# A new order for the work of an attention and gated feed-forward kernel, and a later place for one weight load

## The chip, the cores and the metric

The kernel runs on one core of a Trainium2 chip. A core has five engines that run side by side and meet through semaphores: TensorE (PE in the profile) multiplies matrices and writes to PSUM banks, VectorE (DVE) and ScalarE (ACT) move and change what lies there or in the core's memory, GpSimd (POOL, "Pool" here) does the same without access to PSUM, and SyncE (SP) issues most of the transfers. Pool, SP and ScalarE each have a queue of transfers; all of them run on the same 16 DMA engines. The metric is the device time of one execution, in microseconds (us).

## What is computed

Attention over 4 batches and 8 heads, 768 positions, head size 64, in which each query sees at most six chunks of 32 keys, and behind it a gated feed-forward layer:

```python
k_chunks = k.reshape(B, H, nc, chunk, D)
k_min, k_max = np.min(k_chunks, axis=3), np.max(k_chunks, axis=3)
ub = np.sum(np.maximum(q[:, :, :, None, :] * k_min[:, :, None], q[:, :, :, None, :] * k_max[:, :, None]), axis=-1)
ub = np.where(causal, ub, -1e9)
top_chunks = np.argsort(ub, axis=-1)[..., -6:]        # six chunks by an upper bound of their scores
scores = np.where(selected & not_ahead, q @ k.T / sqrt(D), -1e9)
x = softmax(scores) @ v                               # then heads side by side: 3072 x 512
out = (sigmoid(x @ w_gate) * (x @ w_val)) @ w_out     # 512 -> 1536 -> 512
```

Inputs and outputs are float32; the products run in float16.

## The kernel before

The 24 blocks of 128 query rows (four batches of six) are cut into eight **units** u0 to u7 of three blocks, 384 rows. u0 has the first blocks of batches 0 to 2 (operations named with f: `kfT_0`, `scf_0`, `expf_0_0`, `cmf_0_0`, `pvf_0_0`); each later unit has its own chain:

- keys and queries are loaded (`k0_u2`, `q0_u2`), cast or rearranged (`kn`, `qn`), turned by TensorE (`kT`, `qT`), and copied out as keys (`kt`, `hk`), queries (`qf`, `hq`), positive parts of the queries (`qm`) and smallest and largest keys of each chunk (`kx`, `kcr`);
- `ub` computes the bounds, `ubn`, `mx`, `ap`, `apt` find the sixth largest, `hqm` writes the choice beside the queries;
- `sc` scores, `exp` the exponential, `cm` the causal mask on Pool (line 1014, for u0 `cmf`, line 746), `pv` the product with the values, `rz` and `x` the division, `xps` and `xT` the turn to the layout of the next layer;
- the feed-forward layer: `g` gate products, `tanh` for the sigmoid, `v` value products, `hg` their product, `o` the output product, `osb` its way out of PSUM, `out` the store. From u2 on, the gate and value products are done with seven products of half size instead of eight; for that, **sums of weight blocks** (`ss0_g0` and so on, line 1213) and of the activations (`tt`, line 1226) are needed. Units 4 to 7 do likewise for the output (`tw`, `sw`, `p1` to `p7`).

While the chain of one unit computes bounds and scores, TensorE works on the feed-forward products of the unit before, so the two run interleaved.

What sets the order is written out by hand as three tables. `ORDER` lists all 2013 operations, each with its engine: P TensorE, A ScalarE, V VectorE, G Pool, S SP. Each engine runs its own operations in this order; an operation waits only for what it reads, and for buffers to be free. `SLOTS` gives each buffer its place in memory or its PSUM bank. `TIES` holds pairs `a<b`: operation a (nearly always one of Pool) also waits for the end of b. The tables are used at the end of the kernel:

```python
for op in plan.order():
    op.emit(op.engine)
    for b in ties.get(op.name, ()):
        tc.add_manual_dep(traced[n], ends[b], ..., reason="tie")
```

The weights are loaded by Pool's queue, which casts them to float16. The gate weights come in thirds `wg0` to `wg2`; of the first third, the first quarter of its rows comes alone, earlier, as `wgp` (line 603), so that three gate products of u0 (`ga_u0_0` to `ga_u0_2`) can begin before the rest, `wg0` (line 605), has landed. Between, `fl` are products of ones that keep TensorE running where it has nothing to do. Pool's order at the start is: `epat`, copies of the pattern of chunks into the key buffers (`hkp010`, `hkp100`), `wgp` between these two, then `v10`, the cast `v16_0_0` of the first values (`vf_0`), the masks `cmf_0_0`, `cmf_0_1`, `cmf_1_0`, the cast `vc_1` of the values `vf_1`, `cmf_1_1`, `hkf0`, and then `wg0` and `wv0`.

Of the kernel before, what the change touches and what calls it, by code (L numbers as in the profile page):

```python
# [118 lines left out]
xps_u1_1=P xT_u1_1=A exp_u1_4_2=A hg_u0_6=V hk1_u1_3=V hg_u0_5=V v_u0_8=P g_u0_10=P tanh_u0_10=A kcr1=V hg_u0_10=V g_u0_8=P tanh_u0_8=A  # L119
hg_u0_8=V sc_u1_5_2=P exp_u1_5_2=A g_u0_9=P tanh_u0_9=A hg_u0_9=V sc_u1_4_0=P exp_u1_4_0=A cm_u1_1=G pv_u1_1=P cm_u1_0=G qn_u2_2=G  # L120
sc_u1_5_0=P pv_u1_0=P exp_u1_5_0=A sc_u1_6_1=P exp_u1_6_1=A sc_u1_6_2=P exp_u1_6_2=A exp_u1_5_1=A sc_u1_7_2=P sc_u1_7_0=P g_u0_11=P
qT_u2_2=P sc_u1_7_1=P tanh_u0_11=A exp_u1_7_2=A exp_u1_7_0=A exp_u1_7_1=A kn_u2_1=V kT_u2_1=P rz_u1_0=V x_u1_0=V xps_u1_0=P cm_u1_5=G
pv_u1_5=P cm_u1_4=G pv_u1_4=P qf_u2_2=V q3_u2=S qn_u2_1=V qT_u2_1=P sc_u1_6_0=P kt_u2_1=A exp_u1_6_0=A kn_u2_0=G kT_u2_0=P kt_u2_0=A
v_u0_11=P rz_u1_2=V xT_u1_0=V x_u1_2=V xps_u1_2=P q0_u2=S qn_u2_3=G qT_u2_3=P cm_u1_7=G pv_u1_7=P kx0_u2_0=V o0_u0_0=P o1_u0_0=P
hg_u0_11=V kx1_u2_1=V kx1_u2_0=V cm_u1_6=G pv_u1_6=P rz_u1_3=V x_u1_3=V k2_u2=S qn_u2_0=A qT_u2_0=P o0_u0_1=P xps_u1_3=P xT_u1_3=V
qf_u2_1=A hq0_u2_2=A qf_u2_3=A qm_u2_1=G hq1_u2_1=G k3_u2=S kn_u2_2=G hk1_u2_0=A xT_u1_2=A kT_u2_2=P kn_u2_3=A kT_u2_3=P qf_u2_0=V
# [131 lines left out]
p3z_u67=P e12_u67=A out_u67_0=S  # L258
# [1259 lines left out]
```

## Time and profile before

| | us |
|---|---|
| median of three runs | 273.23 (271.15 to 276.38) |
| the profiled execution | 272.19 |
| its span, first to last instruction | 270.5 |
| busy: TensorE | 261.6 (97%) |
| busy: VectorE | 226.3 (84%) |
| busy: ScalarE | 208.7 (77%) |
| busy: Pool | 181.7 (67%) |

Busy is the union of an engine's instructions in one profiled execution. A matmul's record reaches from its start to the arrival of its last result, so records of neighbours overlap, and a busy TensorE need not be at its full pace. "Idle before" stands with an instruction whose engine did nothing ahead of it, together with what ended the wait. DMA issues on Pool count in its timeline with the time of issuing; the landing comes later. The time of an execution is a little longer than the span, by 1.69 us in the profiled one.

### The profile page before, as it was taken

Reading aid. Unit: us, or ns where it says so; the run is one execution under the profiler, and the core shown is the slowest. Engines: PE = TensorE matmul, PEld = TensorE weight load, DVE = VectorE, ACT = ScalarE, POOL = GpSimd, SP = SyncE. Lnnn points to the kernel's source line nnn. Section 1 sums busy time; section 2 is a strip of 40 time slices with the busy share of each in tenths; the row PEclk is TensorE's granted clock in tenths of the full one; section 3 lists DMA queues with packets and bytes.
Section 4 is the critical chain, followed back from the end, with each engine's and each line's share of the span. In section 5 each row is a group of like instructions: output and inputs, shape, how many; then the busy total and the mean of one; then the engine's idle time right before and its main releaser. Section 6 shows DMA issues by size and latency. Waiting matters only on the chain.

```text
span 270.5 us, 8392 instructions
## 1 busy us (share of the span) xinstructions
PE 261.6 (97%) x3180; PEld 213.1 (79%) x3180; DVE 226.3 (84%) x612; ACT 208.7 (77%) x397; POOL 181.7 (67%) x269
## 2 busy tenths in 40 slices
PE   6888999999999999999999999999999999999994
PEld 4565667656666689886799888889989999999984
DVE  4789946688999999998999998988886889888652
ACT  6269778699999999998988998999976775654221
POOL 5787744677998999867999368476548436770531
PEclk9999999999999999999999999999999999999999
DMA  6999999999999993996955541410100300100236
GB/s 153 228 263 207 203 213 215 235 194 176 188 182 165 212 221 78 185 170 113 204 128 127 135 92 23 130 54 16 33 18 17 82 2 2 40 2 2 78 120 234
DMA packets 131577, 34.76 MB, mean 129 GB/s; under 512 B 119760, under 2 KB 128464, under 8 KB 131536
## 3 DMA queue, kind: packets, MB, share of 16 engines
q1 hardware_dynamic: 125728, 29.24, 51.3%
q0 software_dynamic: 4768, 4.72, 10.4%
q8 instruction: 25, 0.41, 0.7%
q10 hardware_dynamic: 1040, 0.26, 0.4%
q14 instruction: 16, 0.13, 0.1%
HBM read 30.67 MB, written 6.29 MB: 137 GB/s over the span
## 4 chain that ended last, share of the span: by engine, by line
PE 91%; DMA 4%; SPq 1%; POOL 1%; issue 0%; ACT 0%; DVE 0%; POOLq 0%
PE bank L1242 31%; PE bank L991 13%; PE bank L1290 12%; PE bank L1373 11%; PE bank L1135 10%; PE bank L1030 7%; PE bank L912 3%; DMA wg<-in_moe_w_gate_dram 3%; PE bank L702 1%; DMA arena<-in_q_dram 1%; SPq L629 1%; PE bank L788 1%; PE bank L739 0%; POOL arena L746 0%; PE bank L1065 0%
## 5 line engine op out<-in xcount | busy, mean ns | idle before, releaser
L1008 ACT ACTIVATE arena<-bank 128x1024 f16<-128x1024 f32 (+5 forms) x120 | 84.4, 749 | 5.7 <-PE bank L991 4.4
L1242 PE MATMUL bank<-arena 128*128 128x192 f16 x432 | 50.5, 246 | 0.0
L1308 DVE SCALAR_TENSOR_TENSOR arena<-arena,bank 128x384 f16<-128x384 f16 x78 | 41.5, 544 | 10.2 <-ACT arena L1304 4.8
L1125 POOL TENSOR_TENSOR arena<-arena 128x256 f16<-128x256 f16 x39 | 25.4, 669 | 29.8 <-DVE arena L1125 9.5
L1304 ACT ACTIVATE arena<-bank 128x384 f16<-128x384 f32 x78 | 37.4, 493 | 9.2 <-PE bank L1242 4.9
L1014 POOL TENSOR_SCALAR_AFFINE_SELECT arena<-arena 128x384 f16<-128x384 f16 (+1 forms) x56 | 27.5, 503 | 16.7 <-ACT arena L1008 8.5
L1242 PEld LDWEIGHTS <-arena 128*128 128x128 f16 x432 | 36.5, 98 | 2.8 <-issue 0.6
L1373 PE MATMUL bank<-wo,arena 128*128 128x512 f16 x144 | 36.0, 379 | 0.0
L1242 PE MATMUL bank<-arena,wv 128*128 128x192 f16 x288 | 34.0, 246 | 0.0
L1242 PE MATMUL bank<-arena,wg 128*128 128x192 f16 x288 | 32.6, 246 | 0.0
L1030 PE MATMUL bank<-v,arena 128*128 128x65 f16 x640 | 26.8, 193 | 0.0
L991 PE MATMUL bank<-hqo,hko 128*128 128x128 f16 (+2 forms) x220 | 26.5, 243 | 0.0
L991 PE MATMUL bank<-hqe,hke 128*128 128x128 f16 (+2 forms) x220 | 26.4, 243 | 0.0
L1135 PEld LDWEIGHTS <-arena 128*128 128x128 f16 x252 | 24.4, 98 | 2.4
L1030 PEld LDWEIGHTS <-arena 128*128 128x128 f16 x640 | 24.5, 97 | 1.6 <-issue 0.5
L1242 PEld LDWEIGHTS <-wg 128*128 128x128 f16 x288 | 24.3, 98 | 1.6 <-issue 0.4
L1242 PEld LDWEIGHTS <-wv 128*128 128x128 f16 x288 | 24.2, 98 | 1.8 <-issue 0.2
L440 ACT COPY arena<-bank 128x384 f32<-128x384 f32 (+3 forms) x44 | 19.4, 450 | 5.9 <-PE bank L1242 2.7
L1257 DVE TENSOR_TENSOR bank<-bank,arena 128x384 f32<-128x384 f32 x36 | 20.2, 562 | 4.3 <-ACT arena L1304 2.2
L1226 POOL TENSOR_TENSOR arena<-arena 128x384 f16<-128x384 f16 x20 | 18.2, 912 | 6.0 <-DMA arena<-arena 4.3
L1257 DVE TENSOR_TENSOR arena<-bank,arena 128x384 f32<-128x384 f32 x36 | 19.8, 551 | 2.4 <-PE bank L1242 2.1
L1373 PEld LDWEIGHTS <-arena 128*128 128x128 f16 x144 | 13.4, 98 | 10.3
(124 smaller groups left out, 555.8 us busy)
## 6 DMA issues: line engine op xcount, KB each, us to landing
arena<-in_v_dram SPq DMA_DIRECT2D x26, 256.0 KB, 4.0
out_dram<-arena SPq DMA_DIRECT2D x24, 256.0 KB, 2.2
arena<-in_k_dram SPq DMA_DIRECT2D x12, 384.0 KB, 5.6
arena<-in_q_dram SPq DMA_DIRECT2D x12, 384.0 KB, 5.9
arena<-in_q_dram SPq DMA_DIRECT2D x12, 128.0 KB, 5.7
arena<-in_k_dram SPq DMA_DIRECT2D x12, 128.0 KB, 4.2
wv<-in_moe_w_val_dram POOLq DMA_DIRECT2D x3, 512.0 KB, 11.0
wo<-in_moe_w_out_dram POOLq DMA_DIRECT2D x3, 512.0 KB, 15.8
```

The costliest lines, as they stand in the source:

```text
L991: nc.tensor.matmul(at(t)[:, o:o + 128 * m], hk[b % 2][e_][:, p, 128 * jb:128 * jb + 128], hq[u.side][e_][:, p, 128 * x:128 * (x + m)], sta ...
L1008: plan.add(f"exp_{u.name}_{h}_{ys[0]}", {ACT: act(n)}, lambda e, t=t, att=att, b0=b0, n=n: nc.scalar.activation(at(att)[:, b0:b0 + n], at( ...
L1014: nc.gpsimd.affine_select(out=dv, in_=dv, compare_op=ALU.is_ge, fill=0.0, base=0, pattern=[[0, u.m], [1, 128]], channel_multiplier=-1)
L1030: nc.tensor.matmul(at(pv)[:, last, x, :], at(att)[:, c:c + 128], v16[b % 2][:, jb, h, :], start=(jb == 0), stop=(jb == ib))
L1125: plan.add(f"sw{n}_{name}_{j}", {DVE: dve(256, 2), POOL: pool2(256)}, lambda e, a=a, b=b, op=op, n=n, j=j: both(e).tensor_tensor(sums(n, j ...
L1135: nc.tensor.matmul(at(to), a(j)[:, i], b(j)[:, i], start=first and j == i == 0, stop=j == 2 and i == 1, skip_group_check=True)
L1242: nc.tensor.matmul(at(to)[:, s], a()[:, c, 128 * s:128 * s + 128], b()[:, c], start=first and s == c == 0, stop=c == 1, skip_group_check=True)
L1257: plan.add(f"{p}_{name}", {DVE: dve(384)}, lambda e: nc.vector.tensor_tensor(at(f), at(lead), at(f7), ALU.add), reads=[lead, f7], writes=[ ...
L1290: nc.tensor.matmul(at(t), w16[:, c, 128 * fb:128 * fb + 128], at(u.xt)[:, c, :], start=(c == 0), stop=(c == 3))
L1304: plan.add(f"tanh_{u.name}_{name}", {ACT: act(T, psum)}, lambda e: nc.scalar.activation(dst(), src(), AF.Tanh, scale=0.5), reads=reads, wr ...
L1308: plan.add(f"hg_{u.name}_{name}", {DVE: dve(T)}, lambda e: nc.vector.scalar_tensor_tensor(dst(), gate(), 1.0, src(), ALU.add, ALU.mult), r ...
L1373: nc.tensor.matmul(at(o), at(hgs[fc // 2])[:, fc % 2, 128 * tb:128 * tb + 128], wo16[:, fc, lo:hi], start=(fc == 0), stop=(fc == NFB - 1))
```

## The change

Only the three tables change; every operation stays, none is added.

1. `wgp` goes from its place between `hkp010` and `hkp100` to the place between the cast `v16_0_0` and the first mask `cmf_0_0` on Pool.
2. Behind the first eight gate blocks of u0 (`g_u0_4` is the eighth) all of `ORDER` is another one. On TensorE it starts behind `v_u0_8`. 141 operations change engine: 37 from Pool to VectorE and 36 the other way, 19 from ScalarE to Pool and 15 the other way, 19 from VectorE to ScalarE and 15 the other way. Twelve sums of weights (`ss`) stand ahead of the bounds of unit 2 (`ub_u2`), where none stood. The loads of u2 and of the second batch's keys are listed earlier among the other engines' operations; SP's own order is the same up to the first store `out_u0_0`, which now comes behind the loads of the second batch's keys.
3. Behind that point `SLOTS` gives other places, and `TIES` has 178 pairs instead of 159.

```diff
 ORDER = """
...
-ident16=V ap0=V epat=G hkp110=A hkp000=A hkp001=V kT_u1_2=P kcr0=V kt_u1_2=V hk0_u1_2=G vf1_1=G hkp011=V hkp010=G vf1_2=G wgp=G hkp100=G
...
-v10=G vf_0=S v16_0_0=G qf0_2=S qf1_2=S kf0_2=S expf_0_0=A cmf_0_0=G pvf_0_0=P rzf_0_0=V xf_0_0=V kx1_u1_2=V cmf_0_1=G kfT_2=P pvf_0_1=P
+ident16=V ap0=V epat=G hkp110=A hkp000=A hkp001=V kT_u1_2=P kcr0=V kt_u1_2=V hk0_u1_2=G vf1_1=G hkp011=V hkp010=G vf1_2=G hkp100=G kf1_2=S
...
+vf_0=S v16_0_0=G qf0_2=S qf1_2=S kf0_2=S expf_0_0=A wgp=G cmf_0_0=G pvf_0_0=P rzf_0_0=V xf_0_0=V kx1_u1_2=V cmf_0_1=G kfT_2=P pvf_0_1=P
...
-xps_u1_1=P xT_u1_1=A exp_u1_4_2=A hg_u0_6=V hk1_u1_3=V hg_u0_5=V v_u0_8=P g_u0_10=P tanh_u0_10=A kcr1=V hg_u0_10=V g_u0_8=P tanh_u0_8=A
-hg_u0_8=V sc_u1_5_2=P exp_u1_5_2=A g_u0_9=P tanh_u0_9=A hg_u0_9=V sc_u1_4_0=P exp_u1_4_0=A cm_u1_1=G pv_u1_1=P cm_u1_0=G qn_u2_2=G
-sc_u1_5_0=P pv_u1_0=P exp_u1_5_0=A sc_u1_6_1=P exp_u1_6_1=A sc_u1_6_2=P exp_u1_6_2=A exp_u1_5_1=A sc_u1_7_2=P sc_u1_7_0=P g_u0_11=P
...
+xps_u1_1=P xT_u1_1=A hg_u0_6=V hk1_u1_3=V v_u0_8=P q3_u2=S q0_u2=S k2_u2=S k3_u2=S qf1_3=S qf0_3=S vf_3=S kf1_3=S kf0_3=S v_0_5=S v_0_4=S
+sc_u1_5_0=P ss0_g0=G kcr1=V ss0_v1=G cm_u1_0=G exp_u1_4_2=A ss0_v0=V exp_u1_5_0=A g_u0_8=P ss1_g0=V k01_1=S k00_1=S hg_u0_5=V kn_u2_1=G
+qn_u2_2=V ss1_v1=V g_u0_10=P cm_u1_1=G exp_u1_5_1=A tanh_u0_8=A tanh_u0_10=A g_u0_9=P sc_u1_6_0=P kn_u2_0=V g_u0_11=P ss0_v2=G qn_u2_1=A
+tanh_u0_9=A exp_u1_6_0=A ss1_v0=G sc_u1_6_1=P sc_u1_5_2=P pv_u1_1=P exp_u1_5_2=A pv_u1_0=P sc_u1_4_0=P hg_u0_9=V kT_u2_0=P hg_u0_8=V
+hg_u0_10=V tanh_u0_11=A k11_1=S qT_u2_1=P exp_u1_4_0=A cm_u1_4=G qT_u2_2=P qf_u2_2=A k10_1=S rz_u1_0=V cm_u1_6=G kT_u2_1=P kx0_u2_1=V
+o0_u0_0=P kt_u2_1=A kx1_u2_1=V ss3_g0=V x_u1_0=V qf_u2_1=A sc_u1_7_0=P kx1_u2_0=V q11_1=S exp_u1_7_0=A cm_u1_7=G sc_u1_6_2=P sc_u1_7_2=P
+exp_u1_6_2=A ss3_v0=V o0_u0_1=P exp_u1_6_1=A qn_u2_0=A o1_u0_1=P xps_u1_0=P hk0_u2_1=A qT_u2_0=P ss0_g1=V kx0_u2_0=V sc_u1_7_1=P
...
 TIES = """
...
-hqm0_u1_2<hqm0_u1_0 v16_0_3<hg_u0_1 hk1_u1_0<ubm1_u1 v16_0_2<hg_u0_2 v16_0_1<hqm1_u1_0 cm_u1_1<hk1_u1_3 qn_u2_2<kcr1 cm_u1_5<rz_u1_0
-cm_u1_4<x_u1_0 kn_u2_0<qf_u2_2 qn_u2_3<rz_u1_2 cm_u1_7<xT_u1_0 cm_u1_6<x_u1_2 qm_u2_1<hg_u0_11 hq1_u2_1<kx1_u2_0 hq0_u2_1<rz_u1_3
...
+hqm0_u1_2<hqm0_u1_0 v16_0_3<hg_u0_1 hk1_u1_0<ubm1_u1 v16_0_2<hg_u0_2 v16_0_1<hqm1_u1_0 ss0_v1<hg_u0_7 cm_u1_0<rz_u1_1 kn_u2_1<ss1_g0
+cm_u1_1<ss1_v1 ss0_v2<kn_u2_0 cm_u1_7<ss3_g0 cm_u1_5<ss0_g1 kn_u2_3<qf_u2_0 hq0_u2_2<hg_u0_11 ss1_v2<hg_u0_11 hq1_u2_2<ss1_g1
...
```

447 lines of the change are left out of this document (222 added, 225 removed).

## The prediction

> **What bounds the kernel now.** I read the head of the page first, then the busy times by stage, then the list of what TensorE waited for, then its timeline at the places where it did wait. The head says how much each engine has to do:
>
> ```profile
> span 270.5 us, 8392 instructions
> PE 261.6 (97%) x3180; PEld 213.1 (79%) x3180; DVE 226.3 (84%) x612; ACT 208.7 (77%) x397; POOL 181.7 (67%) x269
> PE 91%; DMA 4%; SPq 1%; POOL 1%; issue 0%; ACT 0%; DVE 0%; POOLq 0%
> ```
>
> PE is TensorE. It is busy for 97% of the span and makes up 91% of the chain that ended last. A mean can hide stages, so the same by stages (columns: stretch, its length, then for each engine the busy time and the count of instructions, then the granted clock, the DMA share and GB/s):
>
> ```profile
> 0.00:12.00 12.00, 9.13 (x48) 6.29 (x48) 7.36 (x16) 5.72 (x6) 8.08 (x17) 1.00 0.80 176
> 12.00:24.70 12.70, 10.12 (x108) 7.68 (x107) 10.50 (x31) 9.75 (x21) 11.04 (x20) 1.00 1.10 250
> 24.70:39.00 14.30, 14.27 (x138) 8.90 (x139) 9.17 (x40) 11.53 (x28) 8.66 (x16) 1.00 1.23 205
> 39.00:60.00 21.00, 21.00 (x223) 13.95 (x222) 15.80 (x52) 15.67 (x39) 11.53 (x24) 1.00 1.14 220
> 60.00:100.00 40.00, 40.00 (x411) 27.29 (x409) 38.67 (x79) 38.69 (x65) 35.76 (x42) 1.00 1.08 184
> 100.00:150.00 50.00, 50.00 (x720) 42.84 (x719) 47.63 (x129) 46.18 (x86) 42.09 (x57) 1.00 0.77 147
> 200.00:250.00 50.00, 50.00 (x617) 47.65 (x615) 41.45 (x102) 30.95 (x72) 26.85 (x41) 1.00 0.07 20
> 250.00:267.00 17.00, 17.00 (x159) 15.11 (x156) 10.01 (x32) 4.20 (x12) 7.14 (x11) 1.00 0.35 136
> 267.00:270.50 3.50, 0.07 (x1) 0.00 (x0) 0.31 (x1) 0.38 (x1) 0.00 (x0) 1.00 0.45 174
> ```
>
> From 39 us to 267 us TensorE's busy time equals the stretch, at full clock. What it did wait for (line, releaser, us in total, times, longest) lies before that:
>
> ```profile
> PE bank L702 <- DMA arena<-in_k_dram: 1.5, 2, 0.9
> PE bank L1290 <- ACT arena L440: 0.5, 1, 0.5
> PE bank L1290 <- DMA wg<-in_moe_w_gate_dram: 0.3, 1, 0.3
> ```
>
> Busy can still hide small holes, because matmuls overlap: the next starts before the last one's recorded end. So I checked the pace of starts. The rows (start, us, count) and the group's mean for one instruction:
>
> ```profile
> 37.60 0.81 PE L1290 MATMUL bank<-arena,wg 128*128 128x384 f16 x4
> 124.98 1.89 PE L1373 MATMUL bank<-wo,arena 128*128 128x512 f16 x8
> 264.94 2.13 PE L1135 MATMUL bank<-wo,arena 128*128 128x256 f16 x18
> L1373 PE MATMUL bank<-wo,arena 128*128 128x512 f16 x144 | 36.0, 379 | 0.0
> L1290 PE MATMUL bank<-arena,wv 128*128 128x384 f16 x96 | 18.2, 326 | 0.0
> L1135 PE MATMUL bank<-wo,arena 128*128 128x256 f16 x144 | 19.6, 273 | 0.0
> ```
>
> Eight matmuls of 512 columns take 1.89 us, of which the last 0.379 is its own length: (1.89 - 0.379) / 7 = 216 ns from start to start. The same reckoning gives 161 ns for 384 columns ((0.81 - 0.326) / 3) and 109 for 256 ((2.13 - 0.273) / 17); for the smaller shapes the starts lie 82 (192 columns), 56 (128) and 29 ns (65) apart. Between the first and the last row above stand 2903 matmuls; each shape's count times its pace, with the bounds products (L912) at their own length, comes to 228.4 us, an estimate, against the 229.5 us that passed from 37.60 to 267.07. **So at most about 1.1 us of hidden idle time lies in all that the new order touches**, which on TensorE starts some 4 us behind that first row. Behind 267.07 come one evacuation and the last stores, 3.4 us.
>
> **Part one: the early quarter of the gate weights.** Pool's queue now (rows of its timeline: start, us, line, operation, and in brackets idle time before it and what ended it):
>
> ```profile
> 7.73 0.79 POOL L603 DMA_DIRECT2D wg<-in_moe_w_gate_dram  x1
> 8.58 1.46 POOL L444 COPY hke<-arena 64x1536 f16<-64x1536 f16 x1
> 10.17 0.67 POOL L666 CAST v<-arena 128x512 f16<-128x512 f32 x1
> 11.68 1.22 POOL L746 TENSOR_SCALAR_AFFINE_SELECT arena<-arena 128x512 f16<-128x512 f16 x2 [0.85 <-ACT arena L744]
> 13.30 0.64 POOL L746 TENSOR_SCALAR_AFFINE_SELECT arena<-arena 128x512 f16<-128x512 f16 x1 [0.40 <-ACT arena L744]
> 14.53 0.61 POOL L444 CAST arena<-arena 128x512 f16<-128x512 f32 x1 [0.60 <-DMA arena<-in_v_dram]
> 16.22 0.80 POOL L605 DMA_DIRECT2D wg<-in_moe_w_gate_dram  x1
> 17.02 0.78 POOL L606 DMA_DIRECT2D wv<-in_moe_w_val_dram  x1
> ```
>
> wgp is the first row; it moves to behind the cast at 10.17. What it removes: 0.85 us (7.73 to 8.58) ahead of hkp100. That copy and the cast are no longer late, but the cast waits for the load vf_0, so I leave it at 10.17. What it adds: the same 0.85 us from 10.84 on, which is exactly the 0.85 us for which Pool waits for ScalarE before the first mask at 11.68. That wait is its cover. If the cast slips by some tenths, the masks slip too, and then the 0.40 before the third mask and the 0.60 before the cast of vf_1 take it up: a slip of up to 1.0 us reaches nothing. So the instruction costs 0.
>
> Its DMA counts as well, and SP's loads are what it is moved past:
>
> ```profile
> wg<-in_moe_w_gate_dram POOLq DMA_DIRECT2D x1, 128.0 KB, 5.3
> wv<-in_moe_w_val_dram POOLq DMA_DIRECT2D x3, 512.0 KB, 11.0
> 9.90:12.10 2.20, 2.19 (x20) 1.74 (x20) 1.51 (x4) 1.09 (x2) 1.29 (x4) 1.00 0.93 172
> 12.10:14.50 2.40, 1.42 (x22) 1.22 (x23) 1.14 (x4) 1.71 (x4) 1.43 (x3) 1.00 1.11 293
> ```
>
> It lands 5.3 us after issue, so from 13.0 to about 16.2; its first reader is the block at 23.65 (below), 7 us of cover. The engines are near full in both stretches (0.93, 1.11), so the bytes are only exchanged: SP's loads that land before about 13 us come sooner, those around 15 us come as before. One load of these is on the chain: vf_1, which ends Pool's 0.60 us wait at 14.53. If all of that goes, wg0 is issued 0.6 us sooner than 16.22; if vf_1 still shares the engines with wgp, none of it goes. What TensorE gets from it is read at its own rows:
>
> ```profile
> 23.65 0.75 PE L1290 MATMUL bank<-arena,wg 128*128 128x384 f16 x3 [0.48 <-ACT arena L440]
> 24.73 1.15 PE L1290 MATMUL bank<-arena,wg 128*128 128x384 f16 x6 [0.33 <-DMA wg<-in_moe_w_gate_dram]
> 28.20 0.98 PE L1290 MATMUL bank<-arena,wv 128*128 128x384 f16 x5
> ```
>
> The three early gate products at 23.65 are released by ScalarE, which the change does not touch here, so only the 0.33 us at 24.73 can go. Next is wv0: issued at 17.02, landing 11.0 us on, at 28.02, just ahead of its reader at 28.20; it follows wg0 in the same queue. The step is worth 0 to -0.33; I take -0.2.
>
> **Part two: the new order behind the first eight gate blocks.** It adds and removes no arithmetic: every operation stands in both orders, 73 go from VectorE to Pool or back, 34 from ScalarE to Pool or back, 34 from VectorE to ScalarE or back. For TensorE the sum of paces is the same 228.4 us. So it **cannot gain more than the 1.1 us** above, and any gain in feeding the other engines buys nothing while TensorE is never idle. It can lose: in the old order whatever TensorE needed was there. Lower bound of the step -1.1. For the upper bound I looked at where the new order asks most. Between the eighth gate block (g_u0_4, the row at 37.60) and the bounds of unit 2 (ub_u2), some 18 us of TensorE, twelve of the sums of weights (ss) are pulled forward from the next stage: seven on VectorE, five on Pool.
>
> ```profile
> L1213 DVE TENSOR_TENSOR arena<-wg x3: 384/405/422, 58.7 to 61.4; 128x512 f16<-128x512 f16 x3
> L1213 POOL TENSOR_TENSOR arena<-arena,wv x3: 1150/1152/1155, 65.8 to 90.8; 128x512 f16<-128x512 f16 x3
> L1014 POOL TENSOR_SCALAR_AFFINE_SELECT arena<-arena 128x384 f16<-128x384 f16 x6 | 3.1, 521 | 6.2 <-DVE hko L442 3.5 <-ACT arena L1008 2.6
> L440 ACT COPY arena<-bank 128x384 f32<-128x384 f32 (+3 forms) x44 | 19.4, 450 | 5.9 <-PE bank L1242 2.7
> ```
>
> VectorE: 7 x 0.405 = 2.8 us. Pool: 5 x 1.152 = 5.8 us. ScalarE gets eight instructions more, 8 x 0.450 = 3.6 us. In 39 to 60 us they have 21.00 - 15.80 = 5.2, 9.5 and 5.3 us free, so everything fits; this is the work that hides it. Later, in 60 to 100 us, where VectorE has 38.67 of 40 us, its part of that is taken off it, which buys nothing, as TensorE does not wait for it there. On SP the loads of the second batch's keys now stand ahead of the first store; their readers wait for no load now, so this too is worth 0. If nothing of Pool's five sums were hidden, the step would cost +5.8; with VectorE's too, +8.6. Between -1.1 and +8.6 I take +0.5, near the rows that show no wait at all, because new neighbours give some first waits of tenths.
>
> **Sum.** The profiled execution took 272.19 (its span 270.5 and 1.69 around it), 1.04 under the median of the three runs shown, 273.23. 272.19 - 0.2 + 0.5 = **272.5 us**. Two per cent is about what a measurement of this kernel can tell from no change (the three runs span 271.15 to 276.38).
>
> **Rivals.**
> 1. *Pool becomes late between 40 and 56 us (slower).* The new ties make it possible: the cast kn_u2_1 on Pool waits for VectorE's sum ss1_g0, the mask cm_u1_1 for ss1_v1, the mask cm_u1_0 for rz_u1_1. Pool runs in order, so behind a late kn_u2_1 stand cm_u1_1 and two more sums, and TensorE's pv_u1_1, pv_u1_0 and kT_u2_1 wait for these masks and this cast. It decides from the point where the added 5.8 us find fewer free microseconds than that ahead of the masks: Pool's six masks now have 6.2 us idle before them, so 0.4 us of further lateness is enough. Price 5.8: 278.0; with VectorE's sums 280.8. For it: the margin is thin, 141 operations have changed engine, and the same pattern of ties goes on to the end. Against it: 9.5 us free in the stage. The Trainium skill, SBUF — State Buffer, section "Who interferes with whom", adds that an operation of VectorE with two SBUF inputs and one of Pool that reads SBUF exclude each other; the sums here are such. The trace shows no stretched one (384 to 422 ns, 1150 to 1155 ns).
> 2. *Small losses, under 2%.* Loads that arrive a little late for their new readers, 1 to 5 us together: 273.5 to 277.6. The share of 1.14 and 1.08 of the DMA engines until 100 us speaks for it.
> 3. *wgp does not fit.* Either the cast at 10.17 is late and all covers are used, then the 0.85 us falls on the issue of wg0 at 16.22, and the time is 273.4 with the rest of the sum; or its landing gets much longer in the new place. That costs nothing before 24.73, when wg0 is waited for anyway, so from a landing of 24.73 - 10.84 = 13.9 us on, against 5.3 measured. The Trainium skill, SBUF — State Buffer, section "A bandwidth-pool intuition that's wrong", has a rule that speaks for it: Pool writes the descriptors of such a DMA through a port that VectorE can lock, and a transfer grew from about 620 to 3100 ns. By that factor of five, an estimate, wgp would land 26 us after issue, some 12 us too late. No run here shows it; the 5.3 us stood beside work of VectorE of the same kinds.
> 4. *TensorE's pace is not fixed (faster).* If other neighbours let the 512-column matmuls go at the pace of the 256-column ones, 144 x (216 - 109) ns = 15.4 us go: 256.8. The Trainium skill, TensorE: Matmul & The Clock Gate, section "Back-to-back issue gap", gives 131 ns for 512 columns in a stream. The row of eight above shows 216, whatever stands beside it, and the measurement decides.
>
> **Chances.** Forecast 0.48; rival 2 0.18; rival 3 0.02; rival 1 0.29; faster by over 2% (under 267.8 against the median) 0.03, since the pace would have to change. Within 2%: 0.48 + 0.18 + 0.02 = 0.68. Range: from 270.6 (the lowest run, 271.15, less the 0.33 and a fifth of the hidden 1.1) to 280.8 (rival 1 whole); its own range for the likeliest is 271 to 274.
>
> **What would show it.** Part one: Pool's first mask still near 11.7 us, its cast of vf_1 before 14.53, wg0 issued before 16.22, the row at 24.73 earlier by at most 0.33. Part two: TensorE's busy time equal to the stretch from 39 us to the end, no row of waits with more than tenths, the end of the last matmul near 267. The prediction is wrong if TensorE's waits name Pool (L1014, L444) or VectorE in 40 to 60 us, or a DMA later, or if a matmul shape has another pace.

## The result, and the profile after

The changed kernel takes 276.4 us (median of six runs, 274.5 to 280.0) against 272.16 for the kernel before in the same comparison (six runs, 271.15 to 276.38). The ratio is 1.0147 with a 95% interval of 1.0114 to 1.0181. (The ratio leaves out executions in a slower state of the chip, here the 280.0 and the 276.38, and so is not the ratio of the two medians.) The change makes the kernel slower by about 1.5%, or 4.0 us. That is less than the 2% which the prediction took as the least that a measurement can tell from no change, but the interval tells it clearly. 272.5 was forecast; the result lies inside the wide stated range, above its likeliest part (271 to 274), and in the bracket that was given to the second rival (273.5 to 277.6).

The profiled execution of the changed kernel took 274.5 us, its span 272.7. All lines stand one number higher than before (L1243 is the old L1242). The head of its page, and its line of the chain that ended last:

```profile
span 272.7 us, 8411 instructions
PE 261.9 (96%) x3180; PEld 212.9 (78%) x3180; DVE 225.8 (83%) x609; ACT 207.3 (76%) x397; POOL 182.9 (67%) x272
PE 84%; POOL 3%; DVE 3%; DMA 3%; issue 2%; SPq 2%; ACT 1%; DVEq 0%; POOLq 0%; ACTq 0%
```

TensorE's work is the same (261.9 us against 261.6), but the share of the chain that is TensorE's fell from 91% to 84%: other engines and transfers now end waits. The busy times by stage (columns as before) show in which stages TensorE is no longer full:

```profile
36.48:60.00 23.52, 22.65 (x244) 14.95 (x241) 17.44 (x57) 18.36 (x46) 14.50 (x25) 1.00 1.11 207
60.00:100.00 40.00, 40.00 (x409) 27.33 (x408) 37.52 (x78) 36.95 (x65) 35.18 (x42) 1.00 1.08 192
150.00:200.00 50.00, 49.62 (x733) 41.75 (x730) 44.27 (x135) 43.26 (x70) 32.40 (x48) 1.00 0.25 58
200.00:250.00 50.00, 50.00 (x651) 48.56 (x650) 43.28 (x104) 30.78 (x70) 27.43 (x43) 1.00 0.14 43
268.00:272.70 4.70, 0.04 (x1) 0.00 (x0) 0.00 (x0) 0.38 (x1) 0.00 (x0) 1.00 0.50 190
```

0.87 us are missing between 36.48 and 60, 0.38 between 150 and 200; and behind the last matmul stand 4.7 us in place of 3.4. In the kernel before, TensorE had no wait from 28 us on. Here it had these:

```profile
PE bank L703 <- DMA arena<-in_k_dram: 0.8, 1, 0.8
PE bank L1243 <- DVE bank L1258: 0.4, 1, 0.4
```

The same places in TensorE's timeline, with the eighth gate block (36.48) and the last matmuls (265.91):

```profile
36.48 0.81 PE L1291 MATMUL bank<-arena,wg 128*128 128x384 f16 x4
...
54.10 0.63 PE L703 MATMUL bank<-ident,arena 128*128 128x128 f32 x4 [0.81 <-DMA arena<-in_k_dram]
...
176.12 0.49 PE L1243 MATMUL bank<-arena 128*128 128x192 f16 x4 [0.39 <-DVE bank L1258]
...
265.91 2.13 PE L1136 MATMUL bank<-wo,arena 128*128 128x256 f16 x18
```

With the prediction's sum of paces (228.35 us from the first of these rows to the end of the last) the span falls into three terms: the start of the eighth gate block, what is lost between it and the last matmul's end, and the last part. For the changed kernel the last matmul ends at 265.91 + 2.13 = 268.04, so 268.04 - 36.48 - 228.35 = 3.2 us are lost, and 272.7 - 268.04 = 4.7 us are the last part. The kernel before had 37.60, 1.1 and 3.4. This table holds the same for every kernel that was run (one profiled execution each, us; the ratio is that of its timed runs to those of the kernel before beside them, with interval). new_again and new_third are the changed kernel itself, run again:

| kernel | block at | lost | last part | ratio to before |
|---|---|---|---|---|
| before | 37.60 | 1.1 | 3.4 | |
| changed | 36.48 | 3.2 | 4.7 | 1.0147 (1.0114 to 1.0181) |
| new_again | 38.22 | 3.5 | 4.8 | 1.0152 (1.0117 to 1.0187) |
| new_third | 36.20 | 3.5 | 4.3 | 1.0124 (1.0088 to 1.0161) |
| old_order_late_wgp | 36.96 | 1.5 | 3.4 | 1.0003 (0.9979 to 1.0028) |
| new_order_early_wgp | 36.64 | 2.9 | 4.4 | 1.0116 (1.0087 to 1.0145) |
| new_o2_first | 36.62 | 3.1 | 4.8 | 1.0105 (1.0070 to 1.0140) |
| new_tail_left_out | 36.71 | 3.2 | 3.9 | 1.0092 (1.0060 to 1.0123) |
| new_tail_spread | 36.98 | 4.6 | 4.1 | 1.0085 (1.0052 to 1.0119) |
| new_three_mended | 36.54 | 4.7 | 4.0 | 1.0102 (1.0067 to 1.0137) |
| old_tail_bunched | 37.21 | 1.1 | 3.8 | 1.0024 (1.0001 to 1.0047) |
| new_places | 36.36 | 3.3 | 4.3 | 1.0098 (1.0068 to 1.0129) |
| new_all_mended | 37.63 | 2.1 | 4.2 | 1.0062 (1.0038 to 1.0086) |
| new_places_and_tail | 39.47 | 2.2 | 3.9 | 1.0055 (1.0031 to 1.0079) |

So the loss has two homes. In the three traces of the changed kernel, 2.1 to 2.4 us more than before are lost between the gate blocks and the last matmul, and the last part is 0.9 to 1.4 us longer. Together this is 3.3 to 3.8 us, 1.2 to 1.4% of 272. A single trace tells the middle loss only to about a microsecond: new_order_early_wgp, new_tail_left_out and new_tail_spread have the changed kernel's order, or nearly, up to the last stores, and they lose 1.8 to 3.5 us more than the kernel before. The first column varies by more than a microsecond from execution to execution, whatever the kernel (36.20 and 38.22 are the same kernel).

### The profile page after: what moved, and what is told of

The parts are those of the page before. It is cut to its first block, busy times and chain, and to the rows that moved or that the text cites. A ratio compares the mean times of both kernels' runs of the same rounds, so it can differ in the third digit from the quotient of the medians.

```text
span 272.7 us, 8411 instructions
## 1 busy us (share of the span) xinstructions
PE 261.9 (96%) x3180; PEld 212.9 (78%) x3180; DVE 225.8 (83%) x609; ACT 207.3 (76%) x397; POOL 182.9 (67%) x272
## 4 chain that ended last, share of the span: by engine, by line
PE 84%; POOL 3%; DVE 3%; DMA 3%; issue 2%; SPq 2%; ACT 1%; DVEq 0%; POOLq 0%; ACTq 0%
PE bank L1243 30%; PE bank L1291 11%; PE bank L992 11%; PE bank L1136 10%; PE bank L1374 7%; PE bank L1031 7%; PE bank L913 3%; DMA arena<-arena 2%; SPq L630 1%; PE bank L789 1%; DMA arena<-in_k_dram 1%; POOL arena L555 1%; DVE arena L931 1%; DVE arena L443 1%; DVE arena L762 1%
## 5 line engine op out<-in xcount | busy, mean ns | idle before, releaser
L1243 PE MATMUL bank<-arena 128*128 128x192 f16 x432 | 50.1, 246 | 0.4 <-DVE bank L1258 0.4
L1126 POOL TENSOR_TENSOR arena<-arena 128x256 f16<-128x256 f16 x44 | 28.7, 669 | 22.6 <-DVE arena L1126 8.2
L1243 PEld LDWEIGHTS <-arena 128*128 128x128 f16 x432 | 36.4, 98 | 2.3 <-issue 0.7
L1243 PE MATMUL bank<-arena,wv 128*128 128x192 f16 x288 | 33.7, 246 | 0.0
L1243 PE MATMUL bank<-arena,wg 128*128 128x192 f16 x288 | 32.6, 246 | 0.0
L992 PE MATMUL bank<-hqo,hko 128*128 128x128 f16 (+2 forms) x220 | 27.4, 243 | 0.1
L1243 PEld LDWEIGHTS <-wv 128*128 128x128 f16 x288 | 24.4, 98 | 2.1 <-POOL hqo L445 0.2
L1243 PEld LDWEIGHTS <-wg 128*128 128x128 f16 x288 | 24.2, 98 | 1.8 <-issue 0.6
L1031 PE MATMUL bank<-v,arena 128*128 128x65 f16 x640 | 25.5, 193 | 0.0
L1258 DVE TENSOR_TENSOR bank<-bank,arena 128x384 f32<-128x384 f32 x36 | 20.0, 560 | 3.6 <-ACT arena L1305 1.5
L1258 DVE TENSOR_TENSOR arena<-bank,arena 128x384 f32<-128x384 f32 x36 | 19.6, 549 | 3.1 <-PE bank L1243 1.7
L1227 POOL TENSOR_TENSOR arena<-arena 128x384 f16<-128x384 f16 x16 | 14.8, 932 | 10.0 <-DMA arena<-arena 4.2
```

The lines of the kernel that those rows point to most:

```text
L992: nc.tensor.matmul(at(t)[:, o:o + 128 * m], hk[b % 2][e_][:, p, 128 * jb:128 * jb + 128], hq[u.side][e_][:, p, 128 * x:128 * (x + m)], sta ...
L1031: nc.tensor.matmul(at(pv)[:, last, x, :], at(att)[:, c:c + 128], v16[b % 2][:, jb, h, :], start=(jb == 0), stop=(jb == ib))
L1126: plan.add(f"sw{n}_{name}_{j}", {DVE: dve(256, 2), POOL: pool2(256)}, lambda e, a=a, b=b, op=op, n=n, j=j: both(e).tensor_tensor(sums(n, j ...
L1243: nc.tensor.matmul(at(to)[:, s], a()[:, c, 128 * s:128 * s + 128], b()[:, c], start=first and s == c == 0, stop=c == 1, skip_group_check=True)
L1258: plan.add(f"{p}_{name}", {DVE: dve(384)}, lambda e: nc.vector.tensor_tensor(at(f), at(lead), at(f7), ALU.add), reads=[lead, f7], writes=[ ...
```

## The experiments

**Which part of the change costs.** Three kernels first: the changed one again, the old order with only `wgp` moved, and the new order with `wgp` back in its old place. A fourth moves one output product ahead of the turning of the keys, because the trace named that wait.

```diff
 old_order_late_wgp (against before)
-... hkp010=G vf1_2=G wgp=G hkp100=G
+... hkp010=G vf1_2=G hkp100=G
-... kf0_2=S expf_0_0=A cmf_0_0=G
+... kf0_2=S expf_0_0=A wgp=G cmf_0_0=G
 new_order_early_wgp (against the changed kernel): the same, back
 new_o2_first (against the changed kernel)
-pv_u1_4=P kfT_3=P kf16_3=A o2_u0_0=P qfT_3=P osb_u0_0=A
+pv_u1_4=P o2_u0_0=P osb_u0_0=A kfT_3=P kf16_3=A qfT_3=P
```

> The changed kernel once more, to see in a second profile what its usual time is made of: its profiled execution took 274.5 us, its median 276.4. Theory A (the new order loses at loads, whose landing differs from one execution to the next): ratio about 1.015 to the kernel before, and a profile near 276 us shows TensorE's waits behind 39 us at 3 us or more in place of 1.2, most of them ended by a DMA or by an engine that waited for a DMA. Theory B (the loss is fixed, and the spread is outside the span): the profile has the waits of the first one, 0.8 us at the turn of the keys of f_3 and 0.4 at the side products, and the rest lies outside the span.

> The old order, places and ties; only wgp is moved to its new place on Pool. Theory A: the move alone is a gain: wg0 is issued near 15.3 us in place of 16.22, TensorE reaches the eighth gate block at 36.5 in place of 37.6, and what of these 1.1 us is kept depends on loads at 50 to 54 us that land when they landed before: 271.1 to 271.9 us, ratio 0.996 to 0.999. Rival C (the late wgp holds back later loads and costs): over 273 us, ratio over 1.004.

> The new order, places and ties; only wgp is put back to its old place on Pool. Theory A: TensorE reaches the eighth gate block at 37.6 in place of 36.5, then the 0.8 us wait for the keys of f_3 near 54 us shrinks to 0.1 or nothing, and the time is that of the changed kernel, 276 us, ratio 1.012 to 1.018: the early gain was given back there. Rival C (the move of wgp is what costs): 272 us, ratio 0.998 to 1.002. If the gain was kept: 277.5, ratio 1.019.

> The changed kernel with the output product o2_u0_0 (four matmuls, 0.86 us) ahead of the turn of the keys of f_3, and its evacuation ahead of the cast of these keys. Theory A: the wait of 0.8 us for the load at 54 us falls to 0.1 to 0.2, TensorE reaches the bounds of unit 2 0.4 to 0.8 us sooner, and the time falls by as much, ratio to the changed kernel 0.997 to 0.9985, if nothing behind takes it. If the next loads or the tail take it: no change, 276.4.

Measured: 276.09, 272.01, 274.76 and 275.01 us against 271.62 for the kernel before (19 runs), ratios in the table.

In new_again TensorE's waits from 28 us on come to 1.4 us, of which 1.0 is one wait for VectorE (L1258). So neither theory holds: A asked for 3 us of waits, B for the waits of the first trace. The span is 274.9 us, 2.2 longer than in the first trace, and 1.7 of that lies ahead of the eighth gate block. The load at 54 us came in time there, and the wait near 176 us grew.

The move of `wgp` alone makes no difference that these runs can tell (1.0003; the forecast of -0.2 us would be 0.9993, inside the interval), and the new order keeps its loss without the move (1.0116). Rival C falls, and part two is the loss. Whether the move costs some tenths of a per cent inside the new order is not settled: 1.0116 without it, 1.0124 to 1.0152 with it, and the intervals overlap. The eighth block stood at 36.64 in new_order_early_wgp, where about 37.6 was expected.

With `o2_u0_0` first, nothing stands at `kfT_3`, where the first trace lost 1.0 us (start against pace), and 0.43 at the next turning, `qfT_3`, which waited for a bank that `kx1_u2_3` on VectorE had still to read. But that is no gain of the move: new_again and new_third, without any edit, lose 0.04 or less at `kfT_3` and 0.4 at `qfT_3` too. Which of the two waits appears differs from one execution to the next.

**The last part.** In the new order three half stores are issued late and close together (263.90, 264.32, 264.81 us; before: 261.32, 263.34, 263.84), ahead of the last four. The view of the line of the stores gives the shortest, median and longest time from issue to landing; before, from 263 us on:

```profile
DMA to landing us min/median/max: 2.0/2.0/2.2
```

and in the changed kernel, from 263.5 us on:

```profile
DMA to landing us min/median/max: 2.8/3.0/3.9
```

Three kernels test this: the three stores reduced to one row of 128, the three spread by an earlier `p3z_u45`, and the kernel before with one store moved into a bunch of three.

```diff
 new_tail_left_out (against the changed kernel)
-            out[r:r + 128, lo:hi], src())
+            out[r:r + (1 if name in ("u45_0", "u5_0", "u6_0") else 128), lo:hi], src()[:1] if name in ("u45_0", "u5_0", "u6_0") else src())
 new_tail_spread (against the changed kernel)
-... p3_u45=P c22_u6=V ... out_u5_1=S sw1_u7_2=G sw3_u6_2=G p3z_u5=P e12_u5=V
+... p3_u45=P p3z_u45=P e12_u45=A c22_u6=V ... out_u5_1=S out_u45_0=S sw1_u7_2=G sw3_u6_2=G p3z_u5=P e12_u5=V out_u5_0=S
 old_tail_bunched (against before)
-... p6z_u67=P out_u5_0=S p2_u7=P ... out_u45_0=S out_u7_1=S
+... p6z_u67=P p2_u7=P ... out_u45_0=S out_u5_0=S out_u7_1=S
```

> The changed kernel, in which the three half stores out_u45_0, out_u5_0 and out_u6_0 write only their first row of 128; the other 381 rows' halves are missing from the output. Everything else, the instants of issue too, stays. Theory T (bunched stores): in the new order these three are issued within 0.9 us (263.90 to 264.81), their bytes stand in front of the last four stores in the DMA engines, and so the time from the last matmul's end to the span's end is 4.4 to 4.8 us instead of 3.4. Without the bytes: 3.4 to 3.8, the last store lands 2.0 to 2.2 us after issue instead of 2.8 to 3.0, about 1.0 us off the time, ratio to the kernel before about 1.0115. Rival U (the last evacuations or the end of the program are slower for another reason): the last part stays at 4.4 to 4.8 and the ratio at about 1.015.

> The changed kernel, in which p3z_u45 and e12_u45 come right behind p3_u45, and out_u45_0 and out_u5_0 right behind out_u5_1 and e12_u5, so that the three stores are issued near 261.2, 262.9 and 264.3 us instead of 263.9, 264.3 and 264.8. Theory T: the last part of the span (last matmul's end to the end) falls from 4.4-4.8 to 3.5-3.9 us, the ratio from about 1.015 to 1.0115. Rival U: it stays. If the reordering of TensorE's tail costs a wait of its own, it would show as a later last matmul, by tenths.

> The kernel before with one store moved on SP: out_u5_0 from 261.3 us to behind out_u45_0, so that out_u6_0, out_u45_0 and out_u5_0 are issued within 1.1 us (263.3 to 264.4) and the last four behind them as before. Nothing else is touched. Theory T: the last part of the span grows from 3.4 to 4.0-4.7 us, the landing of the last store from 2.0 to 2.5-2.8, ratio 1.002 to 1.005, with the last matmul where it was. Rival U: 3.4 and 1.000.

The last part fell from 4.3-4.8 to 3.9 us without the bytes and to 4.1 with the stores spread, and rose from 3.4 to 3.8 in the old order with a bunch. (The times alone do not show the first two: 1.0092 and 1.0085 have intervals that overlap with those of the changed kernel.) Landing times of the last stores in new_tail_left_out (one-row stores have none) and in old_tail_bunched:

```profile
DMA to landing us min/median/max: 2.0/2.0/2.4
```

```profile
DMA to landing us min/median/max: 2.0/2.4/2.5
```

The last part missed its expected range in all three: it is 0.1 us above it in new_tail_left_out (3.4 to 3.8), 0.2 above in new_tail_spread (3.5 to 3.9), and 0.2 below in old_tail_bunched (4.0 to 4.7). The parts of the last part show why. The last store is issued 0.44 or 0.45 us behind the last matmul in every trace; then it has to land, and then the span has to end. A transfer has one completion from each of the 16 DMA engines, and the table also says when 15 of the 16 had come (us from the issue of the last store):

| kernel | 15 of 16 | landed | landing to end |
|---|---|---|---|
| before | 1.94 | 1.98 | 0.99 |
| changed | 2.12 | 2.77 | 1.46 |
| new_again | 2.29 | 2.92 | 1.46 |
| new_third | 1.99 | 2.39 | 1.46 |
| new_tail_left_out | 1.95 | 1.98 | 1.46 |
| new_tail_spread | 1.99 | 2.15 | 1.47 |
| old_tail_bunched | 1.99 | 2.00 | 1.36 |

So the extra has two terms. The landing of the last store costs 0.4 to 0.9 us in the three traces of the changed kernel, and without the bytes of the three stores it is gone: that much of theory T holds. The other 0.4 to 0.5 us stand behind the landing in every execution of the new order, whatever the stores do, and make up the whole rise of old_tail_bunched. There SP's closing instructions pause for 0.36 to 0.39 us between two of them, and the kernel before does not; no wait that the trace shows ends this pause, and its cause stays open.

Bunching alone does not make a store late either. In old_tail_bunched the bunched stores landed within 2.3 to 2.5 us and the last one in 2.0, where 2.5 to 2.8 was expected. And in new_tail_spread a store (`out_u6_0`) landed after 4.2 us though it was issued 0.85 us behind the one ahead of it:

```profile
DMA to landing us min/median/max: 2.0/2.4/4.2
```

Fifteen of its 16 completions had come after 2.0 us. In the window of the three stores the view of the DMA queues shows a second party, a load of instructions (columns: packets, MB, share of 16 engines over 263.8 to 268.9 us of the changed kernel):

```profile
q1 hardware_dynamic: 713, 1.31, 67.2%
q8 instruction: 1, 0.02, 1.7%
```

One packet of 16 KB; 1.7% of 16 engines over 5.1 us is 1.4 us on a single engine. It begins at 264.70, in the middle of the bunch, and of the last seven stores all but the one at 264.81 have 15 of their 16 completions within 2.4 us; the sixteenth makes them late. In the kernel before such a packet comes at 263.02, in old_tail_bunched at 262.91, ahead of most of the stores. Bunch and packet together fit all these traces; no run moved the packet alone. More on it below.

**The waits in the middle.** A mending of three places at once:

```diff
 new_three_mended (against the changed kernel): new_tail_spread, new_o2_first, and
-... o2_u3_0=P hqm1_u7_2=V c21_v0_u4=V exp_u6_7_2=A p5_v0_u4=P
+... o2_u3_0=P c21_v0_u4=V hqm1_u7_2=V exp_u6_7_2=A p5_v0_u4=P
```

> The changed kernel with three places of the new order mended together: the tail as in new_tail_spread, the output product o2_u0_0 ahead of kfT_3 as in new_o2_first, and VectorE's c21_v0_u4 ahead of hqm1_u7_2, on which p5_v0_u4 waits near 176 us (0.5 to 1.1 us in the four traces of the new order). If the loss is a sum of separate small waits, they add up: about 1.0 (tail) + 0.4 (loads) + 0.4 (c21) of the 4.1 us, ratio about 1.008 to 1.010. If a wait taken away at one place comes back at the next (a buffer or a load that is late anyway), the ratio stays at 1.011 or above, and the pace curve shows the same loss further on.

The ratio of 1.0102 lies between the two brackets; the trace decides. It lost 4.7 us, more than the changed kernel's 3.2, so the mended waits did not add up to a gain: others took their place. `p5_v0_u4` still lost 0.73 us, and `sc_u7_6_0` lost 1.02 more: it needs Pool's `hq10_u7_2`, which is tied behind the `hqm1_u7_2` that now came later. So the cause lay ahead of both. VectorE's timeline in the changed kernel (start, us, line, operation, and idle time before it):

```profile
172.51 0.57 DVE L443 COPY bank<-bank 128x384 f32<-128x384 f32 x1
173.66 0.98 DVE L958 STREAM_TRANSPOSE arena<-ap 128x768 f16<-128x768 f16 x1 [0.59 <-DMA arena<-arena]
174.56 0.52 DVE L1309 SCALAR_TENSOR_TENSOR arena<-arena,bank 128x384 f16<-128x384 f16 x1
175.11 0.36 DVE L443 COPY hqo<-arena 64x768 f16<-64x768 f16 x1
175.50 0.57 DVE L1258 TENSOR_TENSOR bank<-bank,arena 128x384 f32<-128x384 f32 x1
```

The transpose at 173.66 is `apt_u7`. Its input (`ap_u7`) is ready at 172.37, and still VectorE idles 0.59 us behind the copy that ends at 173.08, until a transfer inside the arena has landed. `SLOTS` says which: the new one puts `apt_u7` at place 4 (768 columns, three places) and `x_u5_3` at place 5. `x_u5_3` is read by `xT_u5_3`, a transposing transfer of SP issued at 169.84, and its place may not be written over before that has landed, here at 173.57. Fifteen of its 16 completions had come by 172.17; the whole idle time is for the sixteenth. Before, `apt_u7` lay at place 25, over queries that no transfer reads any more, and started without any idle time:

```profile
172.28 0.97 DVE L957 STREAM_TRANSPOSE arena<-ap 128x768 f16<-128x768 f16 x1
```

In the eight executions of the new order with these places the idle time was 0.6 to 1.2 us, and behind it stand `hg_u4_000`, `hqm1_u7_2`, `c21_v0_u4` and TensorE's `p5_v0_u4` (0.5 to 1.1 us). `SLOTS` has the same pattern for `x_u4_3` (on `x_u4_1`, read by `xT_u4_1`) and `x_u3_0` (on `x_u3_3`, read by `xT_u3_3`; no loss of TensorE was traced to this one). Three numbers change that:

```diff
 new_places (against the changed kernel), in SLOTS
-x_u3_0:7    x_u4_3:13    x_u5_3:5
+x_u3_0:212  x_u4_3:35    x_u5_3:198
```

> The changed kernel once more, beside the two that follow, as their measure: ratio 1.0147 and 1.0152 so far, so 1.012 to 1.018, and in its trace the wait of p5_v0_u4 near 176 us of 0.5 to 1.1 us again.

> The changed kernel with three numbers of SLOTS changed and nothing else: x_u5_3 to place 198, x_u4_3 to 35 and x_u3_0 to 212. In the new order these buffers lie where a transposing transfer of SP still reads or is still read: apt_u7 is written over x_u5_3, which xT_u5_3 reads until its landing; x_u4_3 over x_u4_1 (xT_u4_1); x_u3_0 over x_u3_3 (xT_u3_3). Theory V (places): VectorE's waits for these landings (0.6 to 1.2 us before apt_u7, up to some tenths before x_u4_3 and x_u3_0) are the cause of TensorE's waits at p5_v2_u3 (0 to 0.6) and p5_v0_u4 (0.5 to 1.1). Then both are gone or under 0.2, the loss from g_u0_4 to the last matmul falls from 3.2-3.5 to 2.0-2.5 us, the ratio by 0.002 to 0.005 against the changed kernel in this call. Rival W (VectorE has too much to do there, the place is only the last of many causes): p5_v0_u4 still waits 0.4 or more, for hg_u4_000 and hqm1_u7_2, and the ratio stays.

VectorE in new_places:

```profile
171.98 0.57 DVE L443 COPY bank<-bank 128x384 f32<-128x384 f32 x1 [0.18 <-PE bank L1243]
172.45 0.97 DVE L958 STREAM_TRANSPOSE arena<-ap 128x768 f16<-128x768 f16 x1
173.59 0.55 DVE L1309 SCALAR_TENSOR_TENSOR arena<-arena,bank 128x384 f16<-128x384 f16 x1 [0.17 <-DMA arena<-arena]
```

`apt_u7` follows at once, and the loss at `p5_v0_u4` fell from 0.57 (new_third, same chip) to 0.14 us. Theory V is right on that place; by the times alone, 1.0098 against 1.0124, no gain of the three numbers is shown, since the intervals overlap. The whole loss of the trace did not fall as expected (3.3 us, 2.0 to 2.5 expected), since two others stood in it: 0.42 at `sc_u5_3_1` and 0.92 at `sc_u7_1_0`, a place that had been quiet in the first traces. The first comes from Pool. Two of its sums (`tt2_u3` and `tt0_u3`) wait for a transfer inside the arena, and the copy `hqm0_u5_2`, which `sc_u5_3_1` needs, is queued behind them; it is so in the changed kernel too, which lost 0.24 us there:

```profile
125.39 1.78 POOL L1227 TENSOR_TENSOR arena<-arena 128x384 f16<-128x384 f16 x2 [4.16 <-DMA arena<-arena]
127.24 0.82 POOL L445 COPY hqe<-arena 64x768 f16<-64x768 f16 x1
```

The second is a shared place again. new_third shows it on ScalarE and TensorE:

```profile
192.08 0.87 ACT L1305 ACTIVATE arena<-bank 128x384 f16<-128x384 f32 x2 [1.70 <-DMA arena<-arena]
...
192.62 0.38 PE L992 MATMUL bank<-hqe,hke 128*128 128x128 f16 x4 [0.83 <-ACT arena L1305]
```

`tanh_u5_210` lies on `x_u6_1`, which `xT_u6_1` reads. Two more kernels mend all that was named, the second with `x_u6_1` at a free place too and without two moves of the first that cost more than they gave:

```diff
 new_all_mended (against the changed kernel): new_places, new_tail_spread, new_o2_first, and
-... kt_u2_1=A kx1_u2_1=V ss3_g0=V x_u1_0=V qf_u2_1=A
+... qf_u2_1=A kt_u2_1=A kx1_u2_1=V ss3_g0=V x_u1_0=V
-... kx0_u2_3=V ss1_g1=V rz_u1_3=V x_u1_3=V ... o2_u0_1=P kx1_u2_3=V
+... kx0_u2_3=V kx1_u2_3=V ss1_g1=V rz_u1_3=V x_u1_3=V ... o2_u0_1=P
-... tt2_u3=G o0_u2_1=P ... tt0_u3=G exp_u4_6_0=A exp_u4_7_0=A hqm0_u5_2=G
+... tt2_u3=G hqm0_u5_2=G o0_u2_1=P ... tt0_u3=G exp_u4_6_0=A exp_u4_7_0=A
 new_places_and_tail: as new_all_mended, without the moves of qf_u2_1 and kx1_u2_3, and in SLOTS
-x_u6_1:10
+x_u6_1:100
```

> The changed kernel with all places mended that the traces name: the three places as in new_places, the tail as in new_tail_spread, o2_u0_0 ahead of kfT_3 as in new_o2_first; besides, ScalarE's qf_u2_1 ahead of kt_u2_1 (sc_u1_7_2 waits 0.23 for its bank), VectorE's kx1_u2_3 ahead of ss1_g1 (qfT_3 waits 0.37 for its bank), and Pool's hqm0_u5_2 ahead of tt0_u3, which waits for a transfer (sc_u5_3_1 waits 0.24 to 0.47 for hqm0_u5_2). If the loss of the change is the sum of these separate waits: loss from g_u0_4 to the last matmul 1.1 to 1.5 us (the kernel before: 1.12), last part of the span 3.9 to 4.1 (before: 3.4), ratio 1.000 to 1.005. If each wait only gives way to the next one: 2.5 us or more lost, ratio 1.008 or more. Under 0.997 would mean that the new order has a gain that the waits hid.

> The changed kernel with four buffers on other places (x_u5_3 198, x_u4_3 35, x_u3_0 212, and x_u6_1 from 10 to 100, on which tanh_u5_210 waited for the transfer xT_u6_1 in two of the traces, 0.9 to 1.0 us at sc_u7_1_0), hqm0_u5_2 ahead of tt0_u3, o2_u0_0 ahead of kfT_3 and the tail as in new_tail_spread; the moves of qf_u2_1 and kx1_u2_3 in new_all_mended are left out, since they cost 0.59 and 0.31 at xps_u1_3 and o0_u0_1. Theory V (the waits of the new order behind 100 us all go back to buffers that a transposing transfer still reads, and its landing takes 2.3 us alone but 3.4 to 4.6 us where a 16 KB instruction load lies in it): behind 100 us nothing over 0.25 is lost at one place; from g_u0_4 to the last matmul 1.6 to 2.0 us, of which about 0.6 at sc_u1_7_2 and qfT_3, last part 4.0 to 4.2; ratio 1.002 to 1.006. If waits of 0.4 or more come up at new places behind 100 us, the theory covers only a part: ratio 1.007 or more.

273.53 against 271.73 us, and 273.17 against 271.82. Behind 100 us neither loses more than 0.3 us at any one place, and the kernel before no more than about 0.2. So theory V holds but for some hundredths (0.28 at `p5_v0_u4`, 0.25 expected), while the body lost 2.1 and 2.2 us, where 1.1 to 1.5 and 1.6 to 2.0 were expected; in new_all_mended the waits before 60 us went to new places (0.58 at `xps_u1_3`, 0.30 at `o0_u0_1`). TensorE's waits from 28 us on in new_places_and_tail are these alone:

```profile
PE bank L703 <- issue: 0.2, 1, 0.2
```

So of the 1.2 to 1.5% some 0.7 to 1.0% went with a bundle: four numbers in `SLOTS`, one operation of Pool, one of TensorE and the order of the last stores. On one chip new_third had 1.0124 (1.0088 to 1.0161) and new_all_mended 1.0062 (1.0038 to 1.0086), which do not overlap. What each part of the bundle gives is not shown by the times. 0.55% stays (1.5 us): about 1 us in the profile's body, of which 0.7 at `sc_u1_7_2` and `qfT_3` (a bank that ScalarE, then VectorE, reads late), and 0.5 in the last part. No version beat the kernel before. (The block of new_places_and_tail stands at 39.47 because TensorE's granted clock was 0.57 between 25 and 29 us in this one execution.)

Across all traces of the new order the shared places follow a simple pattern. Each time that one of the three transfers was late, exactly one of its 16 completions was late; the other 15 had come within 2.33 us. The table gives what TensorE lost behind each place (us), and in how many traces:

| buffer, transfer that it waits for, where the loss stands | shared place, landing in 2.3 us | shared place, late landing | own place, late landing |
|---|---|---|---|
| `x_u4_3`, `xT_u4_1`, at `p5_v2_u3` | 0.01 or less (4) | 0.42 to 0.60 (4, landing 4.1 to 4.4) | 0.01 or less (3, landing 3.9 to 4.5) |
| `apt_u7`, `xT_u5_3`, at `p5_v0_u4` | none | 0.53 to 1.11 (8, landing 3.7 to 4.3) | 0.08 to 0.28 (3, landing 3.7 to 3.9) |
| `tanh_u5_210`, `xT_u6_1`, at `sc_u7_1_0` | 0 (8) | 0.92 to 0.99 (2, landing 4.5) | none |

So neither the shared place nor the late landing costs by itself; the two together do. For the third buffer the own place is not tested, since `xT_u6_1` landed in 2.3 us in new_places_and_tail. Of the other losses, 0.33 and 0.54 at `pv_u5_3` (new_again, new_order_early_wgp) and 0.39 at `o0_u3_2` (new_tail_spread) were not followed to a cause.

## Why the prediction was wrong, point by point

**What failed: the term of part two, +0.5, and its ground.** The step that failed is "I take +0.5, near the rows that show no wait at all". "It can lose: in the old order whatever TensorE needed was there" was right; the search for where it would lose was too narrow. I looked at how much room VectorE, Pool and ScalarE have between 39 and 60 us and found that the work fits. It does fit: the seven sums on VectorE and five on Pool cost what was said (383 to 426 ns but for one of 571, and 1144 to 1157 ns), and no wait of TensorE names them. The loss came from what a sum of busy times cannot show, namely which buffer lies on which, and when the transfer that still reads the place has landed. The diff said that `SLOTS` gives other places; I read it as bookkeeping and gave it no term. Behind 120 us TensorE lost most behind three buffers that lie on a transposing transfer's source, whenever one of the 16 parts of that transfer came late (0.4 to 1.1 us each), and up to 0.5 us behind one copy of Pool (`hqm0_u5_2`) queued after sums that wait for a transfer. Before 60 us it lost 0.6 to 1.2 us to a load that lands after its new reader is ready, or to banks that are read late. In the three traces of the changed kernel the term measured +2.1 to +2.4 us instead of +0.5.

**A second step failed: "Behind 267.07 come one evacuation and the last stores, 3.4 us" was carried over as a constant.** The evacuation is the same (it ends 0.42 us behind the last matmul) and so is the issue of the last store, but landing took 2.4 to 2.9 us instead of 2.0 and the rest 1.46 instead of 0.99. This part grew by 0.9 to 1.4 us. That the last stores stand in another order could be read from the two tables of `ORDER`; nothing there shows the 0.47 us behind the landing, whose cause stays open.

**Loads.** "On SP the loads of the second batch's keys now stand ahead of the first store; their readers wait for no load now, so this too is worth 0" was wrong by one reader: `kfT_3` waits 0.81 us for the last keys of u0's kind (`kf0_3`, landing at 53.97 us, 53.61 before). The load is hardly later; its reader comes earlier. But this is so in the first trace alone of the three: in the other two the load is in time. Rival 2 named such losses, and its bracket holds the result, but only 0 to 1.0 us of the 3.3 to 3.8 are of its kind. That the bracket fits is mostly luck.

**Part one.** -0.2 was forecast; the runs cannot tell it from 0 (ratio 1.0003, interval -0.6 to +0.8 us). Pool's queue did what was said:

```profile
10.12 0.61 POOL L667 CAST v<-arena 128x512 f16<-128x512 f32 x1 [0.34 <-DMA arena<-in_v_dram]
10.67 0.79 POOL L604 DMA_DIRECT2D wg<-in_moe_w_gate_dram  x1
11.72 1.94 POOL L747 TENSOR_SCALAR_AFFINE_SELECT arena<-arena 128x512 f16<-128x512 f16 x3 [0.26 <-ACT arena L745]
13.61 0.61 POOL L445 CAST arena<-arena 128x512 f16<-128x512 f32 x1
...
15.30 0.80 POOL L606 DMA_DIRECT2D wg<-in_moe_w_gate_dram  x1
```

The first mask stands at 11.72 (11.68 before), the cast of `vf_1` at 13.61 (14.53), `wg0` at 15.30 (16.22), and `wgp` lands 5.1 us after issue (in its old place 5.3 before, 4.0 in new_order_early_wgp), so both forms of rival 3 are out. The Trainium skill, SBUF — State Buffer, section "A bandwidth-pool intuition that's wrong", has a rule by which VectorE can hold such a transfer back through a port; no longer landing is to be seen here. `wg0` is issued 0.92 us sooner, more than the 0.6 of the prediction, but not all of that need be the move's: with `wgp` in its old place `wg0` was issued at 16.22 (before) and at 15.63 (new_order_early_wgp, where the cast of `vf_1` had no wait), in its new place at 15.30 and 15.40. That the eighth gate block came 1.12 us earlier in this trace looks like a gain beyond the stated 0.33, but the column of the table shows 36.2 to 38.2 for one and the same kernel.

**Rivals 1 and 4.** No row of waits names Pool in 40 to 60 us, so the 5.8 us of Pool's sums are hidden. TensorE's pace did not change: the last 18 matmuls take 2.13 us in both kernels, and between 200 and 250 us nothing more is lost. The bound "cannot gain more than 1.1 us" was not tested, since no kernel of the new order gained anything.

## What to carry to other kernels

Where an order of work is changed together with the places of its buffers, list for each buffer the last reader of what lay there before; a reader that is a transfer counts until its landing, not its issue, and a wait on it shows as idle time of an engine that has all its inputs. Count that landing not by the usual 2.3 us but by the late ones, up to 4.6 us here: a shared place that costs nothing in one execution costs up to 1 us in the next. Take the last part of a span as a term of its own, and read the order and the spacing of the last stores before calling it constant. A wait that is mended by moving one instruction often passes to the next one in the queue; ask first what the engine ahead of both is idle for.

## What was not expected of the hardware

**A load of instructions seems to delay the transfer that it meets.** The profile's DMA queues show 25 packets of 16 KB on an instruction queue (q8) in each execution; each holds one of the 16 engines for 0.9 to 1.9 us. `xT_u6_1` shows what may come of it in one and the same kernel. Its time to landing, in the changed kernel first and then in new_third:

```profile
DMA to landing us min/median/max: 2.3/2.3/2.3
```

```profile
DMA to landing us min/median/max: 4.6/4.6/4.6
```

In the first, the DMA queues show nothing else between issue and landing. In the second they show, in 187.4 to 192.0 us, one packet of instructions, and 15 of the 16 completions had come after 2.29 us:

```profile
q1 hardware_dynamic: 416, 0.10, 9.6%
q8 instruction: 1, 0.02, 1.3%
```

1.3% of 16 engines over 4.6 us is 0.96 us on one engine. This packet is in flight 2.5 to 3.5 us after issue; most stand earlier. Over all fourteen traces, of the transposing transfers issued behind 130 us, the 53 that had such a packet in flight 1.15 to 1.9 us after issue (a window chosen from the same data) landed in 2.7 to 4.5 us (median 3.7); of the other 165, 144 landed within 2.5 us (median 2.3). Of the 21 late ones among these, to which `xT_u6_1` in new_third belongs, 17 had a packet a little earlier or later, and 4 had none. Of the 144, 29 had one too, over by 1.0 us after issue or begun after 2.18 us. This is an association, strong in all kernels; no run moved an instruction load alone. In 22 of the 74 late ones, among them `xT_u6_1`, exactly one of the 16 completions was late, as if the transfer waited for the one engine that the packet holds. That would explain why the waits at the shared places come and go from execution to execution (0 or 0.9 us at `sc_u7_1_0`). The old order has late transfers behind 130 us too, but none longer than 3.3 us and all 16 parts alike, and TensorE lost nothing to speak of behind them. The Trainium skill, Runtime: NRT & Kernel Launch, section "Instruction fetch mechanics", says that engines refill their instructions in blocks of 16 KiB and that crossing a boundary costs "one DMA tail-bump, mostly hidden"; the size agrees with the packets of this queue, the price does not seem to where another transfer is on the same engine.
